# First two blocks of an attention and two-MoE kernel: another order, other engines, the first two steps in token halves, and identity transposes on an idle TensorE

## The chip, the core and the metric

The kernel runs on one core of a Trainium2 chip, in one launch. The metric is the device time of that launch in microseconds, the median of several runs. Five engines work beside each other, each through its own instructions in order: TensorE (PE), VectorE (DVE), ScalarE (ACT), GpSimd (POOL) and SyncE (SP), which here only issues DMA transfers. PE has a granted clock with two levels, 1.2 and 2.4 GHz; the profile gives it as a share of the higher one.

## The reference

```python
# q, k, v: [8, 8, 576, 64]; per chunk of 64 tokens and head:
scores = q_c @ k_c.T / sqrt(64); scores -= max; attn = exp(scores) / (sum + 1e-9); out = attn @ v_c
x  = out -> [4608, 512]
g  = relu(x @ w_in1)**2;  x1 = g @ w_out1                 # w_in [512, 2048], w_out [2048, 512]
h  = x1 @ w_in2
g2 = (a0 + a1*h + a2*h**2 + a3*h**3) / (1 + |b0|*|h| + |b1|*h**2 + 1e-6);  result = g2 @ w_out2
```

The four weight matrices arrive as 64-bit floats; the kernel loads the two 32-bit words of each and joins them to one 32-bit float.

## The kernel before, in words

The 4608 tokens are 36 attention tiles of 128 tokens and 9 blocks of 512 (4 tiles each). A block goes through 16 steps, one for each 128 columns of the hidden layer. A step `s` has a first product (`mm_h`, L181 to L183 through `mm3`): 12 matmuls of 128x512 into one of two PSUM banks of the pool `hps`; then ACT's Relu and Square (L227, L228), a rounded high part `gh` (L107, DVE) and the low rest `gl` (L110); and, some steps later, a second product (`mm_out1`): 12 matmuls of 128x512 into four `acc` banks. There are 12 because every 128x128 product is done as low x high, high x low and high x high. All 9 blocks pass the first MoE (144 steps), and then all pass the second.

Attention of tile t runs in between: q and k come in (`load_nat`, `load_tok` L253 for the first 8 tiles, `load_qk` L272 in units of 192 tokens and 16 + 16 small DMAs after them), are transposed (L290 with the identity, or L281 on DVE), then scores (`mm_s`, L314), maximum, subtraction, exponential, sum and division (L332 to L347; below: the chain of the tile), the transpose of the result (`f_tr`, L367), its copy out of PSUM (`f_copy`), the product with v (`mm_pv`, L323) and the high and low part of x (`x_evac`: L105, L110). For the first 8 tiles `f_tr`, the transposes of q and k and the scores share PSUM tiles of the pool `aps`; from the second block on this pool has a single tile `a`.

The first MoE's weights are made ready while block 0 and the attention of block 1 run. A weight tile (512 KB) goes through a load by SP (L131 for w_in, L135 for w_out) into a buffer `st`, two ACT operations on its words (L141, L143), a joining on DVE (L148) that frees `st`, a high part (`w_split`: L105 on ACT or L107 on POOL) and a low part on POOL (L110). The first 24 of the 32 tiles share 6 buffers `st`, the last 8 ("late") share 2. So a late load is issued only when the join two tiles before it is done, and behind whatever stands ahead of it in SP's row of DMAs.

What sets the order is a list of events with due times in steps of block 0, sorted, which gives each engine its program order; nothing is reordered after that. Times below 0 are the start: the string `order` lists tile by tile what tiles 0 to 3 do before step 0, and `load_nat` is given a list of loads. In the list `tq0` is the transpose of q of tile 0, `s0` its scores, `f0` its `f_tr`, `pv0` its product with v, `words0`, `join0`, `split0` the work on weight tile 0.

```python
    for i, x in enumerate("q0 k0 q1 k1 q2 k2 v0 q3 k3 v1 w0 v2 w1 v3 w2 w3 w4 q4 k4 w5 q5 k5".split()):
        at(-90 + i, load_nat, x)
```

Of the kernel before, what the change touches and what calls it, by code (L numbers as in the profile page):

```python
# [22 lines left out]
LN_SHIFT = 20  # L23


@with_exitstack
def attn_moe_moe_kernel(
# [60 lines left out]
    T = {}  # L88
    events = []

    def at(t, fn, *args):
        events.append((t, len(events), fn, args))
# [33 lines left out]
    def w_load(n, f, half):  # L126
        w = ((w_in1, w_out1), (w_in2, w_out2))[n][half]
# [10 lines left out]
    def w_words(key):  # L138
        st, pool_ = T[("st",) + key]
# [6 lines left out]
    def w_join(key):  # L146
        st, c = T.pop(("st",) + key)[0], T[("wc",) + key]
# [3 lines left out]
    def w_split(key, eng):  # L151
        _, f, half = key
# [5 lines left out]
    def w_keep(key):  # L158
        _, f, half = key
# [106 lines left out]
    def load_qk(u, src, nm, hp):  # L266
        t0, n = UNITS[u]
# [41 lines left out]
    def mm_s(t, key):  # L309
        q_, k_ = T.pop(("q", t)), T.pop(("k", t))  # L310
# [7 lines left out]
    def mm_pv(t, key):  # L318
        v_, a_ = T.pop(("v", t)), T.pop(("a", t))
        o = banks(T["aps", key], 1)  # L320
        for p in range(HP):
            for c, h in QUARTERS:
                nc.tensor.matmul(out=o[half(h), c, p], lhsT=v_[half(c), 2 * p + h], rhs=a_[h][half(c), :, p],  # L323
                                 start=True, stop=True)
        T["x", t] = o

    def s_max(t):
        m = tl("attn", [128, 32], F32, "m", f"m{t % 2}")[:, 0:2 * HP].rearrange("p (a b) -> p a b", a=2)
        x = T.pop(("s", t))
        T["e", t] = tl("attn", [128, HP, 2, D], F32, "e", f"e{t % 2}")  # L330
        e = T["e", t].rearrange("p b a j -> p a b j")
        nc.vector.tensor_reduce(out=m, in_=x, axis=AX.X, op=ALU.max)  # L332
        nc.vector.tensor_tensor(out=e, in0=x, in1=m.to_broadcast([128, 2, HP, D]), op=ALU.subtract)

    def s_exp(t):
        e = T["e", t]
        nc.scalar.activation(out=e, in_=e, func=ACTF.Exp, scale=scale)

    def s_sum(t):
        z = T["z", t] = tl("attn", [128, 32], F32, "z", f"z{t % 2}")[:, 0:2 * HP].rearrange("p (a b) -> p a b", a=2)  # L340
# [4 lines left out]
    def s_norm(t, eng):  # L345
        e, z = T["e", t].rearrange("p b a j -> p a b j"), T.pop(("z", t))
# [13 lines left out]
    def f_tr(t, pool_="hps"):  # L360
        e = T.pop(("e", t))
        if pool_ == "hps":
            o = h_p.tile([128, HP, 128], F32, name="h", tag="h")
        else:
            o = P["aps"].tile([128, 2, 512], F32, name="a", tag="a")[:, 0].rearrange("p (a j) -> p a j", a=HP)
        for p in range(HP):
            nc.tensor.transpose(out=o[:, p], in_=e[:, p].rearrange("p a j -> p (a j)"), identity=P["ident"])  # L367
        T["aT", t] = o

    def f_copy(t):  # L370
        o = T.pop(("aT", t))
        a = T["a", t] = [tl("attn", [128, 2, HP, 32], F32, "ah", f"at{h}") for h in range(2)]
        for h in range(2):
            for c in range(2):
                copy((nc.scalar, nc.vector)[h], a[h][half(c)].rearrange("p i b r -> p b i r"),
                     o[half(h), :, half(c)].rearrange("p b (i r) -> p b i r", i=2))

    def x_evac(t, eng):
        b, i = divmod(t, TPB)
        xh, xl = (z[:, :, i * 128:(i + 1) * 128].rearrange("p b (c i) -> p c b i", c=2) for z in X[b % 2])  # L380
        x = T.pop(("x", t))
        copy(nc.scalar, xh, x)
        split_lo(eng, xl, x, xh)
# [82 lines left out]
    for i, x in enumerate("q0 k0 q1 k1 q2 k2 v0 q3 k3 v1 w0 v2 w1 v3 w2 w3 w4 q4 k4 w5 q5 k5".split()):  # L466
# [3 lines left out]
    def first(x):  # L470
        nm, t = x[:-1], int(x[-1])
        if nm in ("tq", "tk"):
            tr_nat(t, nm[1] + "n", nm[1])
            tr_copy(t, nm[1], nc.scalar)
# [5 lines left out]
        elif nm in ("norm", "xe"):  # L480
            {"norm": s_norm, "xe": x_evac}[nm](t, {"norm": nc.gpsimd, "xe": nc.vector}[nm])
        elif nm == "split":
            w_split(w_keys[t], (nc.gpsimd, nc.scalar)[t])
        elif nm in ("words", "join"):
            {"words": w_words, "join": w_join}[nm](w_keys[t])
        else:
            {"max": s_max, "exp": s_exp, "sum": s_sum, "f": f_tr, "cp": f_copy}[nm](t)
# [10 lines left out]
    def attention(t, t0):  # L498
        if t < 2 * TPB:
            at(max(t0 - 2.1, 0.45), tr_second, t)  # L500
            at(max(t0 - 1.95, 0.6), tr_copy, t, "q", nc.vector)
            at(max(t0 - 1.95, 0.6), tr_copy, t, "k", nc.vector)
# [5 lines left out]
        at(t0 + 0.2, s_max, t)  # L508
        at(t0 + 0.45, s_exp, t)
# [14 lines left out]
    for t in range(TPB, NTILE + 1):  # L524
# [123 lines left out]
```

## Time and profile before

| | us |
|---|---|
| median of 3 runs (1686.88 to 1687.67) | 1687.42 |
| span of the profiled execution, first to last instruction | 1684.5 |
| PE busy in that span | 1647.5 (98%) |
| DVE, ACT, POOL busy | 1100.5, 927.7, 347.4 |
| first matmul of step 0 (128x512) | at 32.27 |
| mean granted clock of PE | 0.990 |

The span is the measured time less what lies before the first and after the last instruction. In the page's 40 slices PE reads 9 in every slice but the first, second, fourth and last, and the granted clock is below 1 only in the first slice of 42 us. So a reader looks first at where PE stands still or runs slowly, which is in the first 144 us, and there for what ended each wait.

### The profile page before, as it was taken

Reading aid. Unit: us, or ns where it says so; the run is one execution under the profiler, and the core shown is the slowest. Engines: PE = TensorE matmul, PEld = TensorE weight load, DVE = VectorE, ACT = ScalarE, POOL = GpSimd, SP = SyncE. Lnnn points to the kernel's source line nnn. Section 1 sums busy time; section 2 is a strip of 40 time slices with the busy share of each in tenths; the row PEclk is TensorE's granted clock in tenths of the full one; section 3 lists DMA queues with packets and bytes.
Section 4 is the critical chain, followed back from the end, with each engine's and each line's share of the span. In section 5 each row is a group of like instructions: output and inputs, shape, how many; then the busy total and the mean of one; then the engine's idle time right before and its main releaser. Section 6 shows DMA issues by size and latency. Waiting matters only on the chain.

```text
span 1684.5 us, 24455 instructions
## 1 busy us (share of the span) xinstructions
PE 1647.5 (98%) x9312; PEld 1349.8 (80%) x9312; DVE 1100.5 (65%) x1808; ACT 927.7 (55%) x1502; POOL 347.4 (21%) x282
## 2 busy tenths in 40 slices
PE   6898999999999999999999999999999999999998
PEld 5777888888788888888887788888888888888886
DVE  5765765565665556652107877777777777777776
ACT  5663333333333333322447777777777777777775
POOL 2441000000000000000574323232323232323222
PEclk7999999999999999999999999999999999999999
DMA  9644333334334252210431010101010101000000
GB/s 243 177 121 117 81 102 95 88 94 107 79 79 113 71 130 63 71 32 1 137 101 63 1 51 1 50 0 51 1 51 1 51 0 51 1 32 20 1 26 25
DMA packets 213190, 108.58 MB, mean 64 GB/s; under 512 B 182224, under 2 KB 182224, under 8 KB 211920
## 3 DMA queue, kind: packets, MB, share of 16 engines
q1 hardware_dynamic: 213072, 107.01, 23.5%
q8 instruction: 73, 1.20, 0.3%
q14 instruction: 45, 0.37, 0.1%
HBM read 79.69 MB, written 27.26 MB: 63 GB/s over the span
## 4 chain that ended last, share of the span: by engine, by line
PE 87%; DVE 2%; ACT 1%; DMA 0%; issue 0%; SPq 0%; POOLq 0%; POOL 0%; DVEq 0%; ACTq 0%
PE acc L181 15%; PE h L181 14%; PE h L183 14%; PE h L182 14%; PE acc L183 14%; PE acc L182 14%; PE a L323 1%; PE a L314 1%; DVE t L395 1%; DVE w L416 0%; DVE g L421 0%; DMA x2d<-ev 0%; DVE t L415 0%; ACT t L394 0%; ACT gh L105 0%
## 5 line engine op out<-in xcount | busy, mean ns | idle before, releaser
L181 PE MATMUL h<-x,w 128*128 128x512 f32 x1152 | 452.1, 392 | 3.3 <-DVE w L410 2.5
L182 PE MATMUL h<-x,w 128*128 128x512 f32 x1152 | 450.7, 391 | 0.0
L183 PE MATMUL h<-x,w 128*128 128x512 f32 x1152 | 450.1, 391 | 0.0
L110 POOL TENSOR_TENSOR gl<-g,gh 128x512 fp32r<-128x512 f32 x144 | 186.2, 1293 | 550.0 <-ACT gh L105 545.1
L227 ACT ACTIVATE r<-h 128x512 f32<-128x512 f32 x144 | 85.8, 596 | 384.0 <-PE h L183 362.2
L107 DVE CAST gh<-r 128x512 fp32r<-128x512 f32 x144 | 66.0, 458 | 312.1 <-ACT r L228 306.2
L181 PEld LDWEIGHTS h<-x,w 128*128 128x128 f32 x1152 | 217.5, 189 | 50.5 <-DVE w L410 4.5
L183 PEld LDWEIGHTS h<-x,w 128*128 128x128 f32 x1152 | 217.7, 189 | 45.7
L182 PEld LDWEIGHTS h<-x,w 128*128 128x128 f32 x1152 | 217.5, 189 | 45.4 <-DVE x L110 0.4
L181 PE MATMUL acc<-gh,w 128*128 128x512 f32 x576 | 228.8, 397 | 3.0 <-POOL w L110 2.1
L395 DVE SCALAR_TENSOR_TENSOR t<-h,co,t 128x512 f32<-128x512 f32 x144 | 125.4, 871 | 158.3 <-ACT t L394 158.3
L181 PE MATMUL acc<-w,gl 128*128 128x512 f32 x576 | 225.7, 392 | 1.8 <-POOL gl L110 1.8
L183 PE MATMUL acc<-gh,w 128*128 128x512 f32 x576 | 225.0, 391 | 0.0
L182 PE MATMUL acc<-gl,w 128*128 128x512 f32 x576 | 224.9, 390 | 0.0
L183 PE MATMUL acc<-w,gh 128*128 128x512 f32 x576 | 224.2, 389 | 0.0
L182 PE MATMUL acc<-w,gh 128*128 128x512 f32 x576 | 224.1, 389 | 0.0
L110 POOL TENSOR_TENSOR gl<-r,gh 128x512 fp32r<-128x512 f32 x16 | 20.7, 1291 | 681.4 <-DVE gh L107 681.4
L105 ACT ACTIVATE gh<-g 128x512 fp32r<-128x512 f32 x144 | 91.1, 633 | 89.4 <-DVE g L421 89.4
L181 PEld LDWEIGHTS acc<-w,gl 128*128 128x128 f32 x576 | 108.1, 188 | 28.7 <-POOL gl L110 2.6
L181 PEld LDWEIGHTS acc<-gh,w 128*128 128x128 f32 x576 | 108.4, 188 | 28.0 <-POOL w L110 2.3
L183 PEld LDWEIGHTS acc<-gh,w 128*128 128x128 f32 x576 | 108.4, 188 | 23.0
L183 PEld LDWEIGHTS acc<-w,gh 128*128 128x128 f32 x576 | 108.1, 188 | 22.7
(75 smaller groups left out, 2259.7 us busy)
## 6 DMA issues: line engine op xcount, KB each, us to landing
st<-in_moe_w_in_dram SPq DMA_DIRECT2D x32, 512.0 KB, 4.3
st<-in_moe_w_out_dram SPq DMA_DIRECT2D x32, 512.0 KB, 4.2
x2d<-ev SPq DMA_DIRECT2D x36, 256.0 KB, 2.4
x<-x2d SPq DMA_DIRECT2D x9, 1024.0 KB, 4.8
out_dram<-ev SPq DMA_DIRECT2D x36, 256.0 KB, 2.3
v<-in_v_dram SPq DMA_DIRECT2D x32, 256.0 KB, 3.9
w2d<-wc SPq DMA_DIRECT2D x32, 256.0 KB, 2.6
w<-w2d SPq DMA_DIRECT2D x32, 256.0 KB, 2.6
```

The costliest lines, as they stand in the source:

```text
L105: nc.scalar.activation(out=o, in_=x, func=ACTF.Copy)
L107: eng.tensor_copy(out=o, in_=x)
L110: eng.tensor_tensor(out=o, in0=x, in1=hi.bitcast(F32), op=ALU.subtract)
L181: nc.tensor.matmul(out=o, lhsT=al, rhs=bh, start=first and i == 0, stop=False)
L182: nc.tensor.matmul(out=o, lhsT=ah, rhs=bl, start=False, stop=False)
L183: nc.tensor.matmul(out=o, lhsT=ah, rhs=bh, start=False, stop=last and i == len(pairs) - 1)
L227: nc.scalar.activation(out=r, in_=ps, func=ACTF.Relu)
L314: nc.tensor.matmul(out=o[half(c), h, p], lhsT=q_[half(h), p, half(c)], rhs=k_[half(h), p, half(c)], start=True, stop=True)
L323: nc.tensor.matmul(out=o[half(h), c, p], lhsT=v_[half(c), 2 * p + h], rhs=a_[h][half(c), :, p], start=True, stop=True)
L395: nc.vector.scalar_tensor_tensor(out=t, in0=h2, scalar=co[:, 5:6], in1=t, op0=ALU.mult, op1=ALU.add)
```

## The change

- **Order of the start.** The string `order` is written anew: `max`, `sub`, `x_hi`, `x_lo` and the four pieces of `f_copy` become events of their own, with copies of tiles 0 to 3 on other engines (`ON`: "A" ACT, "V" DVE, "G" POOL). The loads are listed anew: v3 stands behind w2, q4, w4 and w5.
- **Halves.** Steps 0 and 1 compute `h` in two halves of 256 tokens (`mm_h_half`): the first halves need tiles 0 and 1 only, and stand before and after `pv3`.
- **Identity transposes.** `warm` puts 20 and then five times 8 transposes of the identity into an unused PSUM tile, between the first transposes of q and k.
- **f_tr.** For tiles 2 and 3 it is 16 products of 64x64 instead of 4 transposes of 128x128. For tiles 4 to 7 it goes into an `hps` bank instead of the tile `a`, and stands earlier among the steps (`t0 + 1.201` instead of `t0 + 1.9`).
- **Engines and due times.** The division of tiles 4 and 6 goes from DVE to POOL, that of tile 3 from POOL to DVE, some high parts and copies change engine, and 43 events (`MOVED`) get another due time, among them the load of the late tile w_out 13.

```diff
+ON = {
+    "cp000": "V", "cp010": "A", "cp110": "A", "cp111": "A", "cp300": "V", "cp401": "V", "cp501": "V",
...
+MOVED = {
+    "w_load:0,4,0": -11.296, "w_words:(0,2,0)": -11.499, "w_join:(0,2,0)": -11.4, "w_words:(0,0,1)": -12.5,
...
     def at(t, fn, *args):
-        events.append((t, len(events), fn, args))
+        key = fn.__name__ + ":" + ",".join(str(x).replace(" ", "") for x in args if isinstance(x, (int, str, tuple)))
+        events.append((t + MOVED.get(key, 0.0), len(events), fn, args))
...
+    def mm_h_half(s, i):
+        for j in range(2):
+            need("w", (0, j, 0), 4)
+            need("x", 2 * i + j, 3)
+        if i == 0:
+            T["h", s] = h_p.tile([128, 512], F32, name="h", tag="h")
+        j = slice(NB // 2 * i, NB // 2 * (i + 1))
+        mm3(T["h", s][:, j], [(w_in_cols(s, c), [X[0][p][:, c, j] for p in range(2)]) for c in range(KC)], True, True)
+
+    def warm(i, n):
+        if i == 0:
+            T["warm"] = P["aps"].tile([128, 2, 512], F32, name="a", tag="s2")
+        for j in range(n):
+            nc.tensor.transpose(out=T["warm"][:, 0, 0:128], in_=P["ident"], identity=P["ident"])
...
-    def f_tr(t, pool_="hps"):
+    def f_tr(t):
+        stage("softmax", t, 5)
         e = T.pop(("e", t))
-        if pool_ == "hps":
-            o = h_p.tile([128, HP, 128], F32, name="h", tag="h")
-        else:
-            o = P["aps"].tile([128, 2, 512], F32, name="a", tag="a")[:, 0].rearrange("p (a j) -> p a j", a=HP)
+        if on(f"fm{t}", "") is not None:
+            o = T["aps", t][:, :, 0:256].rearrange("p a (b j) -> p a b j", j=64)
...
+                        nc.tensor.matmul(lhsT=x, rhs=one, start=True, stop=True, **args)
+            T["aT", t] = o
+            return
+        if t < TPB:
+            o = T["aps", t][:, :, 0:256].rearrange("p a (b j) -> p a b j", j=128)
+        else:
+            o = h_p.tile([128, 512], F32, name="h", tag="h").rearrange("p (a b j) -> p a b j", a=2, j=128)
...
-    for i, x in enumerate("q0 k0 q1 k1 q2 k2 v0 q3 k3 v1 w0 v2 w1 v3 w2 w3 w4 q4 k4 w5 q5 k5".split()):
+    for i, x in enumerate("q0 k0 q1 k1 q2 k2 v0 q3 k3 v1 w0 v2 w1 w2 q4 w4 w5 v3 w3 k5 k4 q5".split()):
...
-    order = """tq0 tk0 s0 tq1 max0 exp0 tk1 s1 sum0 norm0 tq2 max1 tk2 f0 exp1 s2 sum1 norm1 cp0 tq3 pv0 tk3 max2 f1 xe0
-               exp2 sum2 norm2 cp1 s3 pv1 max3 xe1 f2 exp3 words0 sum3 norm3 cp2 join0 pv2 words1 f3 xe2 split0 cp3
-               join1 split1 pv3 xe3"""
+    order = """w020 tq0 w18 tk0 qc0 kc0 w28 s0 max0 tq1 sub0 w38 qc1 tk1 exp0 w48 kc1 s1 sum0 max1 norm0 sub1 tq2 qc2 exp1 f0
+               cp00 cp03 tk2 kc2 sum1 w58 cp01 s2 cp02 norm1 pv0 max2 sub2 xr0 xh0 xl0 tq3 qc3 exp2 f1 cp10 cp12
+               cp11 cp13 tk3 kc3 s3 sum2 max3 norm2 sub3 words0 xr1 pv1 xh1 join0 split0 xl1 exp3 words1 sum3
+               norm3 f2 cp20 cp22 cp21 cp23 join1 split1 pv2 xr2 xr3 xh2 f3 cp30 cp32 cp31 cp33 half00 pv3 xl2
+               half10 xh3 xl3"""
...
-            at(t0 + 0.8, s_norm, t, nc.vector)
-            at(t0 + 1.9, f_tr, t, "aps")
-            at(t0 + 1.95, f_copy, t)
+            at(t0 + 0.8, s_norm, t, on(f"norm{t}", "V"))
+            at(t0 + 1.201, f_tr, t)
...
     for s in range(NS):
-        at(s, mm_h, s)
+        if s < 2:
+            at(s, mm_h_half, s, 1)
+        else:
+            at(s, mm_h, s)
```

In `order`, `w020` is `warm(0, 20)`, `cp03` is the piece 3 of `f_copy` of tile 0, `half10` is the first half of step 1.

SP's row, the loads of the start before (`v` is the load of v of tiles 1, 2 and 3, `st` a weight tile):

```order
DMA v<-in_v_dram 128x8x64
DMA st<-in_moe_w_in_dram 128x2x512
DMA v<-in_v_dram 128x8x64
DMA st<-in_moe_w_in_dram 128x2x512
DMA v<-in_v_dram 128x8x64
DMA st<-in_moe_w_in_dram 128x2x512 x2
```

The same place after:

```order
DMA v<-in_v_dram 128x8x64
DMA st<-in_moe_w_in_dram 128x2x512
DMA v<-in_v_dram 128x8x64
DMA st<-in_moe_w_in_dram 128x2x512 x2
DMA qn<-in_q_dram 64x8x64 x2
DMA st<-in_moe_w_out_dram 128x1024 x2
DMA v<-in_v_dram 128x8x64
```

The load of v of tile 3 has moved from behind two weight tiles to behind five and q of tile 4.

PE's row around `f_tr` of tile 4 before; it stands behind the second product of step 1 (`w_1`), and writes the tile `a`:

```order
L181 MATMUL acc_516<-gh,w_1_91 128x512
L182 MATMUL acc_516<-gl,w_1_91 128x512
L183 MATMUL acc_516<-gh,w_1_91 128x512
L367 MATMUL a<-ident,e 128x128 x4
L181 MATMUL h<-x_69,w_4_80 128x512
```

After, it stands behind the first product of step 3, and writes an `hps` bank:

```order
L221 MATMUL h<-x_70,w_3_79 128x512
L222 MATMUL h<-x_69,w_3_79 128x512
L457 MATMUL h<-ident,e 128x128 x4
L353 MATMUL a<-ident,qn 128x128 x4
L353 MATMUL a<-ident,kn 128x128 x4
L220 MATMUL acc_621<-gh,w_1_91 128x512
```

So it comes one product of 12 matmuls earlier, ahead of the transposes of q and k of tile 5, which stood far ahead of it.

SP's row at the late weights before (`qs`, `ks` are the small loads of q and k of a unit, `st` of w_out the late tiles 11, 12 and 13 to 15):

```order
DMA qs<-in_q_dram 32x6x32 x4
DMA st<-in_moe_w_out_dram 128x1024
DMA qs<-in_q_dram 32x6x32 x12
DMA st<-in_moe_w_out_dram 128x1024
DMA ks<-in_k_dram 32x6x32 x16
DMA st<-in_moe_w_out_dram 128x1024 x3
```

The same place after:

```order
DMA qs<-in_q_dram 32x6x32 x4
DMA st<-in_moe_w_out_dram 128x1024
DMA qs<-in_q_dram 32x6x32 x8
DMA st<-in_moe_w_out_dram 128x1024
DMA ks<-in_k_dram 32x6x32 x4
DMA st<-in_moe_w_out_dram 128x1024
DMA ks<-in_k_dram 32x6x32 x12
DMA st<-in_moe_w_out_dram 128x1024 x2
```

Tile 12 stands behind 8 small loads instead of 12, and tile 13 behind 4 instead of 16; 12 of them now stand ahead of tile 14.

## Rows read from the trace of the kernel before

**Rows 1.** Stretches (us): length, busy and count by engine, granted clock, DMA share, GB/s.
```profile
0.00:10.00 10.00, 5.09 (x48) 3.94 (x48) 1.38 (x2) 3.09 (x5) 0.70 (x6) 1.00 0.92 178
10.00:20.00 10.00, 6.29 (x155) 5.03 (x154) 7.08 (x15) 6.05 (x13) 2.09 (x2) 1.00 1.03 256
20.00:30.00 10.00, 5.44 (x79) 3.88 (x73) 7.05 (x16) 5.43 (x11) 3.96 (x4) 0.52 1.00 249
30.00:40.00 10.00, 8.86 (x57) 7.02 (x58) 3.87 (x7) 7.18 (x13) 4.40 (x4) 0.63 1.03 293
144.00:880.00 736.00, 735.02 (x4840) 603.50 (x4839) 394.99 (x784) 248.68 (x424) 54.89 (x43) 1.00 0.34 86
```

**Rows 2.** Timeline, PE and POOL at the start: start, duration, engine, line, [idle before, releaser].
```profile
1.01 0.29 POOL masks.py:199 TENSOR_SCALAR_AFFINE_SELECT ident<-ident 128x128 f32<-128x128 f32 x1
4.21 1.09 PE L290 MATMUL h<-ident,qn 128*128 128x128 f32 x4 [4.21 <-DMA qn<-in_q_dram]
...
8.17 1.11 PE L290 MATMUL h<-ident,qn 128*128 128x128 f32 x4
9.08 1.06 PE L290 MATMUL h<-ident,kn 128*128 128x128 f32 x4
...
30.31 1.13 PE L323 MATMUL a<-ah,v 64*64 64x64 f32 x30 [0.83 <-DVE ah L107]
32.27 0.76 PE L181 MATMUL h<-x,w 128*128 128x512 f32 x1 [0.83 <-ACT x L105]
...
37.62 0.60 PE L290 MATMUL a<-ident,qn 128*128 128x128 f32 x4
38.06 0.60 PE L290 MATMUL a<-ident,kn 128*128 128x128 f32 x4
```

**Rows 3.** Timeline, PE, block 0 with the attention of tiles 4 to 8.
```profile
49.08 0.63 PE L290 MATMUL a<-ident,qn 128*128 128x128 f32 x4 [1.09 <-issue]
...
57.37 0.63 PE L367 MATMUL a<-ident,e 128*128 128x128 f32 x4 [1.76 <-DVE k L107]
...
79.27 0.63 PE L367 MATMUL a<-ident,e 128*128 128x128 f32 x4 [2.69 <-DVE k L107]
...
120.39 0.63 PE L367 MATMUL a<-ident,e 128*128 128x128 f32 x4 [1.08 <-ACT r L228]
123.08 0.79 PE L181 MATMUL acc<-gh,w 128*128 128x512 f32 x1 [2.06 <-POOL w L110]
...
126.22 0.40 PE L182 MATMUL acc<-gl,w 128*128 128x512 f32 x1
...
132.58 0.39 PE L183 MATMUL acc<-gh,w 128*128 128x512 f32 x1
137.16 1.14 PE L323 MATMUL a<-ah,v 64*64 64x64 f32 x32 [4.19 <-DVE ah L107]
138.89 1.13 PE L314 MATMUL a<-k,q 64*64 64x64 f32 x32 [0.60 <-DVE k L281]
...
143.42 0.40 PE L183 MATMUL h<-x,w 128*128 128x512 f32 x1
```

**Rows 4.** Timeline, SP's row of DMAs and ACT at the late weights.
```profile
120.67 7.64 SPq L272 DMA_DIRECT2D ks<-in_k_dram  x16
128.41 9.62 SPq L135 DMA_DIRECT2D st<-in_moe_w_out_dram  x3
...
132.49 0.66 ACT L141 ACTIVATE wc<-st 128x512 f32<-128x512 f32 x1 [5.66 <-DMA st<-in_moe_w_out_dram]
```

**Rows 5.** Timeline, scores (PE) and division (DVE) of tiles 5 and 6.
```profile
63.92 0.65 PE L314 MATMUL a<-k,q 64*64 64x64 f32 x32
76.03 0.69 DVE L347 TENSOR_TENSOR e<-e,z 128x512 f32<-128x512 f32 x1
88.53 0.65 PE L314 MATMUL a<-k,q 64*64 64x64 f32 x32
95.97 1.52 DVE L347 TENSOR_TENSOR e<-e,z 128x512 f32<-128x512 f32 x1
```

More of the change, by code (lines that the diff above doesn't have):

```diff
@@ L88, in attn_moe_moe_kernel, with on, stage, need @@
     T = {}
+    engines = {"A": nc.scalar, "V": nc.vector, "G": nc.gpsimd, "": None}
+    def on(what, usual):
+        return engines[ON.get(what, usual)]
     events = []
     def at(t, fn, *args):
-        events.append((t, len(events), fn, args))
+        key = fn.__name__ + ":" + ",".join(str(x).replace(" ", "") for x in args if isinstance(x, (int, str, tuple)))
+        events.append((t + MOVED.get(key, 0.0), len(events), fn, args))
+    done = {}
+    def stage(what, key, i):
+        if done.get((what, key), 0) != i:
+            raise ValueError(f"{what} {key}: stage {i} out of order")
+        done[what, key] = i + 1
+    def need(what, key, i):
+        if done.get((what, key), 0) < i:
+            raise ValueError(f"{what} {key} is not at stage {i}")
     def issue(until):
@@ L126, in w_load @@
     def w_load(n, f, half):
+        stage("w", (n, f, half), 0)
         w = ((w_in1, w_out1), (w_in2, w_out2))[n][half]
@@ L138, in w_words @@
     def w_words(key):
+        stage("w", key, 1)
         st, pool_ = T[("st",) + key]
@@ L151, in w_split @@
     def w_split(key, eng):
+        stage("w", key, 3)
         _, f, half = key
@@ L158, in w_keep @@
     def w_keep(key):
+        stage("w", key, 3)
         _, f, half = key
@@ L186, in mm_h @@
         b, f = divmod(s, NF)
+        if s < NS:
+            for i in range(2):
+                need("w", (0, f // 2 * 2 + i, 0), 4)
+            for i in range(TPB):
+                need("x", b * TPB + i, 3)
+        stage("h", s, 0)
         ps = h_p.tile([128, 512], F32, name="h", tag="h")
@@ L266, in load_qk @@
     def load_qk(u, src, nm, hp):
+        stage(nm, u, hp)
         t0, n = UNITS[u]
@@ L280, in tr @@
         for u, to, of, n in units(t):
+            need(nm, u, HP)
             nc.vector.transpose(
@@ L309, in mm_s @@
     def mm_s(t, key):
+        stage("s", t, 0)
         q_, k_ = T.pop(("q", t)), T.pop(("k", t))
@@ L318, in mm_pv @@
     def mm_pv(t, key):
+        if t < TPB:
+            for i in range(4):
+                stage(f"copy{i // 2}{i % 2}", t, 1)
+        else:
+            stage("softmax", t, 10 if t < 2 * TPB else 6)
         v_, a_ = T.pop(("v", t)), T.pop(("a", t))
@@ L368, in f_tr, with f_copy @@
         T["aT", t] = o
[L370 to L378, printed above, removed]
-        b, i = divmod(t, TPB)
[L380 to L383, printed above, removed]
+    def f_copy(t, h, c):
+        stage("softmax", t, 6 + (2 * h + c if t >= TPB else 0)) if t >= TPB else stage(f"copy{h}{c}", t, 0)
+        if on(f"fm{t}", "") is not None:
+            if h == 0 and c == 0:
+                a = tl("attn", [128, HP, 2, D], F32, "ah", f"at{t % 2}")
+                copy(on(f"cp{t}{h}{c}", "A"), a.rearrange("p (a b) h j -> p a (b h) j", a=2), T["aT", t])
+                T["a", t] = [a[:, :, h_] for h_ in range(2)]
+            return
+        if h == 0 and c == 0:
+            T["a", t] = [tl("attn", [128, HP, D], F32, "ah", f"at{h_}") for h_ in range(2)]
+        copy(on(f"cp{t}{h}{c}", "AV"[h]), T["a", t][h][half(c)].rearrange("p (a b) j -> p a b j", a=2),
+             T["aT", t][half(h), :, :, half(c)])
@@ new lines, in x_parts, with x_raw, x_hi @@
+    def x_parts(t):
+        b, i = divmod(t, TPB)
+        return [z[:, :, i * 128:(i + 1) * 128].rearrange("p b (c i) -> p c b i", c=2) for z in X[b % 2]]
+    def x_raw(t):
+        stage("x", t, 0)
+        if t >= 2 * TPB:
+            need("h", (t // TPB - 1) * NF - 1, 1)
+        if (eng := on(f"xr{t}", "")) is not None:
+            x = x_parts(t)[1].bitcast(F32)
+            copy(eng, x, T.pop(("x", t)))
+            T["x", t] = x
+    def x_hi(t):
+        stage("x", t, 1)
+        copy(on(f"xh{t}", "A"), x_parts(t)[0], T["x", t])
@@ L387, in t2, with x_lo @@
+    def x_lo(t):
+        stage("x", t, 2)
+        xh, xl = x_parts(t)
+        split_lo(on(f"xl{t}", "V"), xl, T.pop(("x", t)), xh)
     def t2(nm):
```

69 lines of the change are left out of this document (53 added, 16 removed), and 13 rows, old and new, of tables (MOVED, ON).

## The prediction, put down before the changed kernel ran

> **What bounds the kernel now.** I read the stretches first. From 144 to 880 us PE is busy 735.02 of 736 us at the full clock [rows 1], and nothing in the change touches what runs there. So the question is only when PE comes to the work that both kernels do alike from about 144 us on; each microsecond won or lost before that goes through to the end. Before 144 us the granted clock is about half from 20 to 30 us and 0.63 from 30 to 40 us [rows 1], and the timeline of PE shows where it waits.
>
> Of this I make a budget, from the first matmul of step 0 at 32.27 us on.
>
> Waits of PE [rows 2, 3], in the order of time: 1.09 (transposes of tile 5, which need the tile `a`), 1.76 and 2.69 (`f_tr` of tiles 4 and 5, held by the copy of k out of the same tile `a`), 1.08 (`f_tr` of tile 7), 2.06 (a late weight's low part on POOL), 4.19 (product with v of tile 7) and 0.60. Together 13.5 us.
>
> Slow clock. At the full level a 128x512 matmul takes (132.58 - 126.22) / 28 = 0.227 us, for 28 starts between these rows [rows 3]. The 12 matmuls of step 0 take 37.62 - 32.27 = 5.35 us [rows 2] where 12 x 0.227 = 2.73 would do: 2.6 lost. The seven from 123.08 to 126.22 take 3.14 against 1.59: 1.55 lost. From 137.16 to 143.42 pass 6.26 us, less 0.60 of waiting 5.66, for a product with v, scores and eight matmuls, which at the full level are about 2 x 0.6 + 1.8 = 3.0 [rows 3]: 2.6 lost. Together 6.8 us. Waits and slow clock after 32.27 us make 20.3 us: that is what can be won there.
>
> The longest wait shows where it comes from. SP issues 16 small loads of k for 7.64 us from 120.67 on, and only then w_out 13. ACT waits 5.66 us for that landing, until 132.49, and what stands behind it on ACT (Relu of a step, a copy of tile 7's transposed result) waits with it, and so the product with v at 137.16 [rows 3, 4].
>
> **The change part by part.**
>
> *The start.* Step 0 can't end before tile 3 has its product with v, and v3 now comes later. Ahead of and with v3 stand 13 loads of 256 KB and five of 512 KB, 6.0 MB. The queue moved 1.8 MB in the first 10 us, 2.6 in the next, and 2.5 in the third [rows 1]: v3 can't land before about 27 us. The new identity transposes cost something: the identity is there at 1.3 us, four transposes at the pace of 8 to 9 us take 9.08 - 8.17 = 0.91, so the first 20 end at 1.3 + 20 x 0.23 = 5.9 us and hold the first real ones, which started at 4.2, as soon as q0 had landed [rows 2]. Loads into the buffer of q0 wait for those. That moves the loads by up to 1.7 us. I take 29 us for v3, with 27 and 31 as ends. From its product with v to the first matmul of step 0 pass 32.27 - 30.31 = 1.96 us [rows 2], so the second half of step 0 starts at 31 (29 to 33). By then the first halves of steps 0 and 1 are done, in the time in which PE stood idle before: 12 x 0.227 = 2.73 us of work. Before, this point was 32.27 + 2.73 = 35.0. Won: 4.0 us (2 to 6). The other new work on PE there (40 identity transposes, 32 products of 64x64 in place of 8 transposes) lies in the stage that waits for loads and for the chain of the tiles; I cost it at nothing, and at its own 40 x 0.11 to 40 x 0.23 = 4 to 9 us if that cover were gone.
>
> *Halves.* 48 matmuls of 256 columns take the place of 24 of 512. No row shows one. A 128-column transpose has a pitch of (38.06 - 37.62) / 4 = 0.11 [rows 2], a 512-column one 0.227. Ends: half of 0.227, so nothing lost, or all of it, 24 x 0.114 = 2.7 us for the two halves behind the wait for tile 3. As a load of 128 columns of weights fits into 0.11, I take 0.12 and 0.4 us in all.
>
> *Clock at the start.* PE is slow from 20 us on because it has little to do, and rose again 3 to 6 us after it got dense work: at 37.6 after 32.27, at 126.2 after 123.08, at 143.4 after 137.16 [rows 2, 3]. The last eight identity transposes stand before the scores of tile 2, so nothing new fills the stretch in which the clock fell. The first halves start the dense work about 2 to 3 us earlier, partly under waits. At this level (1.2 GHz) the second halves would take 5.4 us instead of 2.7. I leave 1.5 us lost (0 to 2.6).
>
> TensorE: Matmul & The Clock Gate of the Trainium skill says (What's actually happening) that the throttled state is the default and activity releases it. By that rule more transposes are good anywhere in the start, and the 1.5 us would be 0. The trace agrees that dense work releases it, but shows the full level already at 38 us only and not where the transposes were added; the second rival below takes the rule's side.
>
> *f_tr of tiles 4 to 7.* It no longer needs the tile `a`, so the waits of 1.09, 1.76 and 2.69 lose their cause. But it comes earlier, so the chain of its tile must be done earlier; where it isn't, PE waits, and all products behind it with it. Before, the division of tile 5 ended at 76.72, 12.2 us after its scores (64.57), that of tile 6 at 97.49, 8.3 us after (89.18) [rows 5]. Now PE has, between scores and `f_tr`: for tile 4 three groups of 12 matmuls, 8.2 us; for tile 5 three and two transposes and a product with v, 9.5; for tile 6 two and the transposes, 6.3; for tile 7 two and a product with v, 6.0. The chains get shorter: DVE takes the maximum of tile 5 behind fewer joins, tile 6 loses a join (0.6) and its division goes to POOL. I work them out at about 7 to 8 us, so tile 6 waits 1.1 and the others little. For this, and for a wait for k4 (0.7) and for the first weight of the second product (0.5), which both come a little late when PE is 5 us ahead, I take 3 us (0 to 12).
>
> *Late weights.* w_out 13 now stands behind 4 small loads, 12 fewer, each 7.64 / 16 = 0.48: 5.7 us earlier, the length of ACT's wait [rows 4]. w_out 12 is 1.9 us earlier. Since SP sends the small loads also earlier where PE is ahead (the joins that free its buffers stand at the same place among the steps), I expect the 2.06, 4.19 and 0.60 gone, and with them the two slow stretches. What is late next is w_out 14, behind 12 small loads, 5.7 us; it is first used three groups later (8 us), so it is covered.
>
> **The sum.** 20.3 + 4.0 - 0.4 - 1.5 - 3 = 19.4 us. The profiled span of 1684.5 becomes 1665.1. The median of the runs is 2.9 above the span, so 1668. The most that the terms allow is 20.3 + 6 = 26.3 us, 1661; the least, with 12 us of new waits, 2.7 for the halves, 2.6 of slow clock and 2 won at the start, is 5 us, 1682, but not all of these ends come at once.
>
> **The rivals.**
>
> *New waits at f_tr.* If the chains keep their length, 8.3 to 12.2 us, mean 10.3, the four tiles wait 2.1, 2.7, 2.0 and 4.3 = 11 us in place of my 1.1. For it: DVE and ACT still run strictly by program order, and Relu and joins stand before the maximum. Against: the copies and joins that stood there are moved. Time: 1668 + 10 = 1678.
>
> *The transposes keep the clock up.* Then nothing is slow at the start: 1666.5. Against it: the clock had risen by 37 us and earlier without them, and fell where none is added.
>
> *Late weights come no earlier.* If SP, not PE, sets the pace of the late tiles, then 2.06 + 4.19 + 0.60 and the 4.2 of slow clock stay: 1668 + 11 = 1679. For it: the last tiles share two buffers. Against it: PE's first wait of 2.06 comes when these loads stand behind small ones, and that is what moves.
>
> *Slower: the two `hps` banks.* `f_tr` now takes one of the two banks, so the next first product needs the bank of the step just before, which ACT's Relu frees; and Relu stands in ACT's row behind words of weights that may not have landed. A wait like the one of 5.66 us [rows 4] would then stop PE directly. Four of these are 22.6 us in place of my 3. After the waits of 2.06 and 4.19 the clock fell, at 1.55 and 2.6 us; four times 2.1 make 8.4 more: 1668 - 3 + 22.6 + 8.4 = 1696. It decides where wait and slow clock together pass (19.4 + 3) / 4 = 5.6 us for each of the four tiles, a wait of 3.5 us. Against it: in block 0 the weights are loaded far ahead, so only the last two could meet it.
>
> **How the numbers follow.** Forecast 0.57; new waits at `f_tr` 0.19; clock kept up 0.08; late weights no earlier 0.08; slower by the banks 0.08. The time is that of the likeliest, 1668. The range holds the likeliest, the second and the third rival and all but the far end of the first: 1661 to 1680. This measurement can tell about 0.2% (3.4 us) from no change. Faster by more: nearly all of the first four cases, less 0.06 for cases that end near zero because several of the smaller terms go wrong together: 0.86. Within: 0.06. Slower: 0.08.
>
> **What would show it.** Right: in the profile after, the first matmul of 256 columns stands at 26 to 29 us and the second half of step 0 at 29 to 33; the waits of `f_tr` for the copy of k are gone; no wait of ACT for w_out over 2 us; no granted clock below 1 after 40 us; PE comes to the step that ran at 144 us about 20 us earlier. Wrong: waits of 2 us or more in front of the transposes of tiles 4 to 7 (first rival); a first product that waits for Relu (the last); ACT still waiting 5 us for w_out 13; or the second half of step 0 later than 34 us, since then the loads at the start were mis-sized.

## The result, and the profile after

The changed kernel takes 1670.74 us (median of 4 runs, 1670.36 to 1670.81) against 1687.15 for the kernel before beside it: a ratio of 0.9904 with a 95% interval from 0.9890 to 0.9918, 16.4 us less. The forecast was 1668 with a range from 1661 to 1680. The span of the profiled execution is 1668.9 us, 15.6 below the 1684.5 of before.

The page after: the span, the busy time, and the slices of PE and of its granted clock.

```profile
span 1668.9 us, 24673 instructions
...
PE 1649.8 (99%) x9436; PEld 1356.2 (81%) x9436; DVE 1101.5 (66%) x1806; ACT 923.9 (55%) x1494; POOL 353.4 (21%) x286
...
PE   8989999999999999999999999999999999999998
...
PEclk8999999999999999999999999999999999999999
```

A 9 in the row of the clock stands for 90% or more of a slice. The page of before has a 9 there for the slow stretches at 120 to 126 us (0.73) and 135 to 145 us (0.66) too, so its clock was below 1 in more than the first slice.

The same stretches as in [rows 1], columns as there:

```profile
20.00:30.00 10.00, 8.50 (x107) 7.60 (x97) 6.96 (x13) 6.42 (x12) 4.18 (x5) 0.56 1.14 270
30.00:40.00 10.00, 9.98 (x123) 9.12 (x123) 5.35 (x9) 7.62 (x14) 4.58 (x5) 0.93 1.12 283
144.00:880.00 736.00, 734.38 (x4835) 602.57 (x4833) 390.02 (x769) 252.33 (x429) 61.63 (x48) 1.00 0.34 86
```

From 144 to 880 us PE is as full as before: 734.38 of 736 us busy. What was won lies before. In this execution the clock is 0.93 from 30 to 40 us in place of 0.63; from 20 to 30 us it is still near half, though PE is now busy 8.50 us instead of 5.44.

Where the time came from is read off one mark that both kernels have, the scores of tiles 4 to 9 on PE (start, us, by the timelines):

| scores of tile | 4 | 5 | 6 | 7 | 8 | 9 |
|---|---|---|---|---|---|---|
| before | 41.61 | 63.92 | 88.53 | 110.27 | 138.89 | 161.26 |
| after | 37.47 | 57.09 | 79.44 | 101.61 | 124.00 | 145.08 |
| lead | 4.1 | 6.8 | 9.1 | 8.7 | 14.9 | 16.2 |

So 4.1 us come from the start, 5.0 from the stretch between the scores of tiles 4 and 6, and 7.5 from that of the late weights (tiles 7 to 9); 0.4 is lost between. Each row is one execution. Among the experiments below, the runs with the start of the kernel before have the scores of tile 4 at 41.6 to 43.0 us (five executions with this one), and those with the start of the changed kernel at 36.9 to 38.6 (six): in the mean the start is worth 4.4 us, and a single pair of profiles gives it only to within about 1.5 us.

The timeline of PE at the start (start, duration, line, [idle before, releaser]), with the half steps on L220 to L222:

```profile
1.36 3.76 PE L249 MATMUL a<-ident 128*128 128x128 f32 x20 [1.36 <-POOL ident masks.py:199]
4.96 0.60 PE L353 MATMUL h<-ident,qn 128*128 128x128 f32 x4
...
25.59 1.06 PE L447 MATMUL a<-ident,e 64*64 64x64 f32 x8
26.58 1.96 PE L449 MATMUL a<-ident,e 64*64 64x64 f32 x16
28.47 0.58 PE L220 MATMUL h<-x,w 128*128 128x256 f32 x1
...
30.99 0.41 PE L222 MATMUL h<-x,w 128*128 128x256 f32 x1
31.33 0.75 PE L392 MATMUL a<-ah,v 64*64 64x64 f32 x32
...
33.54 0.28 PE L220 MATMUL h<-x,w 128*128 128x256 f32 x1
...
34.86 0.28 PE L222 MATMUL h<-x,w 128*128 128x256 f32 x1
34.98 0.60 PE L353 MATMUL a<-ident,qn 128*128 128x128 f32 x4
...
37.47 0.69 PE L378 MATMUL a<-k,q 64*64 64x64 f32 x32
```

The first half of step 0 runs from 28.47, the product with v of tile 3 comes behind it at 31.33, and at 33.54, behind the first half of step 1, the second half of step 0 begins (forecast 29 to 33, so it is 0.5 us past the end of that range; the first half was forecast at 26 to 29). From 25.59 on PE doesn't wait for anything: it is busy with the 64x64 products and the half step, at half clock until about 31.4.

The waits of PE in block 0 with the attention of tiles 4 to 8, to be laid beside [rows 3]:

```profile
51.41 0.50 PE L220 MATMUL h<-x,w 128*128 128x512 f32 x1 [0.76 <-ACT r L288]
...
87.38 0.65 PE L457 MATMUL h<-ident,e 128*128 128x128 f32 x4 [0.75 <-POOL e L423]
...
110.36 0.63 PE L457 MATMUL h<-ident,e 128*128 128x128 f32 x4 [1.90 <-DVE e L423]
118.31 0.50 PE L220 MATMUL h<-x,w 128*128 128x512 f32 x1 [1.86 <-ACT r L288]
124.00 0.69 PE L378 MATMUL a<-k,q 64*64 64x64 f32 x32
```

All seven waits of [rows 3], 13.5 us, are gone; four new ones of 5.3 us stand there. Two are `f_tr` (L457) waiting for its tile's division, two are a first product (L220) waiting for Relu (L288), that is, for its `hps` bank. From 31.4 to 160 us the granted clock is 1.00 in this execution.

SP and ACT at the late weights, beside [rows 4]:

```profile
109.58 1.83 SPq L334 DMA_DIRECT2D ks<-in_k_dram  x4
111.51 0.39 SPq L170 DMA_DIRECT2D st<-in_moe_w_out_dram  x1
111.94 6.81 SPq L334 DMA_DIRECT2D ks<-in_k_dram  x12
118.84 2.27 SPq L170 DMA_DIRECT2D st<-in_moe_w_out_dram  x2
```

```profile
96.17 0.67 ACT L177 ACTIVATE wc<-st 128x512 f32<-128x512 f32 x1 [2.45 <-DMA st<-in_moe_w_out_dram]
...
116.56 0.67 ACT L177 ACTIVATE wc<-st 128x512 f32<-128x512 f32 x1 [1.99 <-DMA st<-in_moe_w_out_dram]
...
122.43 0.67 ACT L177 ACTIVATE wc<-st 128x512 f32<-128x512 f32 x1 [1.06 <-DMA st<-in_moe_w_out_dram]
```

The load of w_out 13 stands behind 4 small loads, and ACT's wait for it, at 116.56, has shrunk from 5.66 to 1.99 us.

### The profile page after: what moved, and what is told of

Same layout as the page of the kernel before. It is cut to its first block, busy times and chain, and to the rows that moved or that the text cites. A ratio compares the mean times of both kernels' runs of the same rounds, so it can differ in the third digit from the quotient of the medians.

```text
span 1668.9 us, 24673 instructions
## 1 busy us (share of the span) xinstructions
PE 1649.8 (99%) x9436; PEld 1356.2 (81%) x9436; DVE 1101.5 (66%) x1806; ACT 923.9 (55%) x1494; POOL 353.4 (21%) x286
## 4 chain that ended last, share of the span: by engine, by line
PE 91%; DVE 3%; ACT 2%; DMA 1%; SPq 1%; issue 1%; POOL 0%; POOLq 0%; DVEq 0%; ACTq 0%
PE acc L220 15%; PE h L220 15%; PE h L222 15%; PE h L221 15%; PE acc L222 14%; PE acc L221 14%; PE a L392 1%; SPq L334 1%; PE a L378 1%; DMA st<-in_moe_w_out_dram 1%; DVE t L506 1%; DVE w L527 1%; DVE g L532 0%; PE a L249 0%; DVE t L526 0%
## 5 line engine op out<-in xcount | busy, mean ns | idle before, releaser
L220 PE MATMUL h<-x,w 128*128 128x512 f32 (+1 forms) x1160 | 452.7, 390 | 5.1 <-ACT r L288 2.6
L221 PE MATMUL h<-x,w 128*128 128x512 f32 (+1 forms) x1160 | 450.8, 389 | 0.0
L222 PE MATMUL h<-x,w 128*128 128x512 f32 (+1 forms) x1160 | 450.7, 389 | 0.0
L288 ACT ACTIVATE r<-h 128x512 f32<-128x512 f32 x144 | 85.8, 596 | 383.6 <-PE h L222 361.3
L220 PEld LDWEIGHTS h<-x,w 128*128 128x128 f32 x1160 | 218.7, 188 | 52.6 <-DVE w L521 4.5
L222 PEld LDWEIGHTS h<-x,w 128*128 128x128 f32 x1160 | 218.8, 189 | 44.9
L220 PE MATMUL acc<-gh,w 128*128 128x512 f32 x576 | 228.0, 396 | 1.1 <-DVE ev L141 0.8
L220 PE MATMUL acc<-w,gl 128*128 128x512 f32 x576 | 225.7, 392 | 2.0 <-POOL gl L144 1.7
L222 PE MATMUL acc<-gh,w 128*128 128x512 f32 x576 | 224.5, 390 | 0.0
L222 PE MATMUL acc<-w,gh 128*128 128x512 f32 x576 | 224.2, 389 | 0.0
L220 PEld LDWEIGHTS acc<-w,gl 128*128 128x128 f32 x576 | 108.1, 188 | 29.2 <-issue 2.9
L220 PEld LDWEIGHTS acc<-gh,w 128*128 128x128 f32 x576 | 108.1, 188 | 25.7 <-DVE ev L141 1.6
L222 PEld LDWEIGHTS acc<-gh,w 128*128 128x128 f32 x576 | 108.1, 188 | 22.8
L222 PEld LDWEIGHTS acc<-w,gh 128*128 128x128 f32 x576 | 108.1, 188 | 22.6
```

Source lines behind the costliest of these rows:

```text
L220: nc.tensor.matmul(out=o, lhsT=al, rhs=bh, start=first and i == 0, stop=False)
L221: nc.tensor.matmul(out=o, lhsT=ah, rhs=bl, start=False, stop=False)
L222: nc.tensor.matmul(out=o, lhsT=ah, rhs=bh, start=False, stop=last and i == len(pairs) - 1)
L288: nc.scalar.activation(out=r, in_=ps, func=ACTF.Relu)
```

## The experiments

Each was timed beside the kernel before on the same chip (1686.4 to 1686.7 us); "of before" is the ratio with its interval. Differences from the changed kernel of less than about 2 us aren't resolved, since the changed kernel itself read 1670.74 and, repeated, 1671.51 us (0.9906 [0.9892, 0.9921]):

> The changed kernel once more, beside the others on the same chip: 1670 to 1672 by its first runs.

In the profile of the repeat, PE waits as long at `f_tr` of tile 7 as in the first one (1.90 there), but the wait of 1.86 us for Relu behind it isn't there:

```profile
110.78 0.63 PE L457 MATMUL h<-ident,e 128*128 128x128 f32 x4 [1.89 <-DVE e L423]
```

Instead the granted clock is 0.50 from 112 to 115 us.

**One: three due times of late loads taken out of the changed kernel.**

```diff
-    "load_qk:1,qs,0": -0.523, "load_qk:1,qs,1": -0.641, "w_load:0,13,1": -0.494,
```

> The changed kernel, with the three due times taken back that moved small loads of q and k of the second unit and the load of w_out 13: 16 small loads stand ahead of w_out 13 again. If the late weights' place in SP's row is what removed the waits behind w_out 13: w_out 13 is issued some 3 to 4 us later than at 111.5, ACT waits for it by so much more, PE waits 3 to 4 us more before a first product or a product with v, and the clock falls behind it: 1674 to 1677 us. If the pace of the late tiles is set elsewhere (the two buffers): within 1 us of 1670.7, since w_out 11 and 12 come about 2 us earlier in this order.

Measured: 1677.61, 0.9945 of before [0.9930, 0.9959], 6 to 7 us above the changed kernel and 0.6 above the expected range. The timeline of its PE and of its ACT:

```profile
123.17 0.80 PE L220 MATMUL h<-x,w 128*128 128x512 f32 x1 [8.33 <-ACT r L288]
```

```profile
121.43 0.66 ACT L177 ACTIVATE wc<-st 128x512 f32<-128x512 f32 x1 [6.89 <-DMA st<-in_moe_w_out_dram]
122.54 0.58 ACT L288 ACTIVATE r<-h 128x512 f32<-128x512 f32 x1
```

ACT waits 6.89 us for w_out, Relu stands behind it, and PE waits 8.33 us for the bank that Relu frees, 6.5 more than the 1.86 of the changed kernel, where 3 to 4 more were expected. The granted clock is 0.50 from 120 to 126 us. So the late loads are worth 6 to 7 us in the changed kernel, and the mechanism of the "slower" rival exists.

**Two: the same three due times alone, put into the kernel before.**

```diff
+        if fn.__name__ == "load_qk" and args[0] == 1 and args[2] == "qs" and args[3] < 2:
+            t -= (0.523, 0.641)[args[3]]
+        if fn.__name__ == "w_load" and args == (0, 13, 1):
+            t -= 0.494
```

> The kernel before, with the three due times alone that move eight small loads of q and the load of w_out 13. If these due times alone take away what I counted for the late weights (waits of 2.06, 4.19 and 0.60 and 4.2 of slow clock): 11 us faster, 1676. My own expectation after taking them back in the changed kernel (6.9 us): w_out 11 now stands behind four more small loads (1.9 us later) where it was already 2.06 us late, so 1.9 us are lost there and 4.19 + 0.60 + 2.6 won: 5.5 us faster, 1680 to 1683.

Measured: 1681.71, 0.9969 [0.9959, 0.9979]: 5.0 us faster.

**Three: the `hps` bank for `f_tr` of tiles 4 to 7 alone, in the kernel before, at the old place.**

```diff
-            at(t0 + 1.9, f_tr, t, "aps")
+            at(t0 + 1.9, f_tr, t)
```

> The kernel before, with f_tr of tiles 4 to 7 in an hps bank instead of the tile a, at its old place among the steps. If the copy of k out of the tile a is what held it: the waits of 1.76 and 2.69 go, 4.5 us, 1682 to 1683.5, and the clock and the late weights stay. If taking one of the two banks makes the first products wait for Relu for as long: 1686 or more, with waits of h for ACT's Relu of 2 us or more.

Measured: 1688.37, 1.0008 [0.9998, 1.0017]: nothing. The waits for the copy of k (1.76 and 2.69 us) are gone, and first products wait instead, as the timeline of PE shows:

```profile
58.66 0.77 PE L181 MATMUL h<-x,w 128*128 128x512 f32 x1 [2.38 <-ACT r L227]
...
79.89 0.50 PE L181 MATMUL h<-x,w 128*128 128x512 f32 x1 [0.55 <-ACT r L227]
...
133.67 0.79 PE L181 MATMUL h<-x,w 128*128 128x512 f32 x1 [5.88 <-ACT r L227]
```

Everything that the free tile `a` gave was given back at the bank.

**Four: both of these, and then the earlier place of `f_tr` as well** (`t0 + 1.201` for `t0 + 1.9`).

> The kernel before with the three earlier due times of late loads and with f_tr of tiles 4 to 7 in an hps bank, at its old place. By themselves they gave -5.0 and +1.6 us. First theory, they need each other (the bank's wait of 5.9 us at tile 7 was a Relu behind words of w_out 13, which now land earlier; and the copy of k no longer holds f_tr): 1676 to 1680, no wait of a first product for Relu over 3 us. Second theory, they add up: 1682.5 to 1685, with the 5.9 us still there or moved.

> The same, with f_tr of tiles 4 to 7 also at its new place (due 1.2 steps behind the scores), engines and joins as in the kernel before. First theory, the place needs the shorter chains that the other edits make: f_tr waits for the division of tiles 4 to 7 by 6 to 11 us together, and the time is 3 to 8 us above that of the run with the bank and the loads alone. Second theory, the place alone does it: waits at f_tr of 3 us or less, 1674 to 1678, and the rest of the change outside the start is worth 2 us or less.

Measured: 1681.51 (0.9969 [0.9957, 0.9980]) and 1681.84 (0.9973 [0.9963, 0.9983]), the same as the late loads alone. The first lies between the times of its two theories (1676 to 1680, 1682.5 to 1685): the 5.88 has become 0.87, as the first theory had it; but the wait at tile 4 stays, the clock is at its lower level behind it (0.50 from 60 to 62 us), and 1.71 (division of tile 7) and 2.07 (a late weight) come in. PE and then ACT of the first:

```profile
59.77 0.64 PE L185 MATMUL h<-x,w 128*128 128x512 f32 x1 [2.35 <-ACT r L231]
```

```profile
57.41 0.63 ACT L109 ACTIVATE w<-wc 128x512 fp32r<-128x512 f32 x1 [2.51 <-DVE wc L152]
...
59.06 0.57 ACT L231 ACTIVATE r<-h 128x512 f32<-128x512 f32 x1
```

Here Relu is late because ACT's row has the high part of a weight ahead of it, which waits 2.51 us for a joining on DVE. In the second kernel `f_tr` comes too early for the old chain of its tile; these waits come to 6.8 us, as its first theory had it, without the 3 to 8 us of time that it forecast (PE):

```profile
53.48 0.63 PE L371 MATMUL h<-ident,e 128*128 128x128 f32 x4 [2.96 <-DVE e L351]
...
120.83 0.63 PE L371 MATMUL h<-ident,e 128*128 128x128 f32 x4 [3.17 <-DVE e L351]
```

So neither bank nor place is worth anything without the other order and engines. What the bank is worth with them was not run: no run has the new order and engines with `f_tr` in the tile `a`. Against the changed kernel the second one is 4.5 us behind at the scores of tile 4 (41.99), loses 5.5 more up to those of tile 5 (67.07), and in each stretch after that the two differ by 0.7 us at most. Of these 5.5 us, 4.0 are two waits (2.96 above and 1.07 before the transposes of tile 5), and about 1.7 are an estimate for the clock, which is 0.50 from 54 to 57.4 us; the changed kernel has one wait of 0.76 us there.

**Five: only the place of `f_tr` undone in the changed kernel** (back to `t0 + 1.9`, in the `hps` bank, and without the four entries of `MOVED` for `f_tr` of tiles 4 and 6 and a copy of tiles 4 and 7).

> The changed kernel with f_tr of tiles 4 to 7 back at its old place (due 1.9 steps behind the scores in place of 1.2), still in an hps bank. First theory, the place is what lets the bank be free again: the waits for the division (0.75 and 1.90 us) go, but a first product now stands right behind f_tr of tiles 4, 5 and 7 or one group after it, and waits for Relu as in the kernel before with the bank alone (2.4, 0.6 and 5.9 us there): 1673 to 1677. Second theory, Relu is no longer behind words of weights, so the place is worth nothing: 1669 to 1671.5.

Measured: 1672.39, 0.9914 [0.9899, 0.9929]: 0.9 to 1.7 us above the changed kernel, not resolved, and between the ranges of the two theories. Its waits at the bank are 0.74 and 0.21 us, and one of 2.32 us for a late weight's low part comes in. The second theory is nearer: with the new engines the place is worth less than these runs resolve.

**Six: the halves undone, steps 0 and 1 whole.**

> The changed kernel with steps 0 and 1 as whole first products of 512 columns behind tile 3, as before. If the halves hide work in a stage in which PE has time: the product with v of tile 3 comes 2.5 us earlier, because the first half no longer stands before it, step 0 starts at about 31, and after it 2.7 us more of first products are to be done, part of them at the slow clock: 1672 to 1673.5. If the halves hide all their work: 2.7 us or more lost, over 1673.5. If PE was not what the second halves waited for: 1670.7.

Measured: 1672.60 (1670.31 to 1675.79), 0.9917 [0.9902, 0.9932]: 1.1 to 1.9 us above the changed kernel, not resolved. PE at the start:

```profile
30.27 1.13 PE L392 MATMUL a<-ah,v 64*64 64x64 f32 x32 [2.23 <-DMA v<-in_v_dram]
32.19 0.77 PE L220 MATMUL h<-x,w 128*128 128x512 f32 x1 [0.80 <-ACT x L139]
```

Without the first half in between, the product with v of tile 3 waits for its load, which landed at 30.2 us, and the scores of tile 4 come at 41.13. Against the profile of the changed kernel the halves are worth 3.7 us there (2.5 to 4.3 against the six executions of its start), of which 1.3 are left at the scores of tile 9 (146.35): a PE that comes later finds more of what it would wait for done, and waits 2.9 us in all between 33 and 160 us instead of 5.3.

**Seven: `f_tr` of tiles 2 and 3 as four transposes of 128x128 again** (`fm2` and `fm3` out of `ON`).

> The changed kernel, with four 128x128 transposes for f_tr of tiles 2 and 3 as before, in place of 16 products of 64x64. In the changed kernel these two groups hold PE for 2.5 and 2.9 us (21.01 to 23.5 and 25.59 to 28.47). If PE's slow work there holds the start: f_tr takes about 0.9 us each, the first halves start 2 to 3 us earlier, the second halves 1 to 2.5 us earlier, 1668.5 to 1669.7. If the four copies in place of one and the load of v3 (landed 27.43) hold it, or the clock rises later because PE does less: 1670 to 1672.

Measured: 1671.50, 0.9909 [0.9894, 0.9924]: no difference. PE:

```profile
26.67 1.13 PE L392 MATMUL a<-ah,v 64*64 64x64 f32 x32 [4.42 <-DVE ah L141]
27.73 1.11 PE L457 MATMUL a<-ident,e 128*128 128x128 f32 x4
```

`f_tr` of tile 3 now takes 1.11 us in place of 2.9, but the four copies out of PSUM that this form needs hold the product with v of tile 2 by 4.42 us (0.75 in the changed kernel), and the first half begins at 28.50. The longer form on PE buys one copy instead of four; the two are even within what these runs resolve.

**Eight: all 60 identity transposes out.**

> The changed kernel without its 60 identity transposes. If they only raise the clock from 4 us on instead of 10, while the first transposes start 0.75 us earlier without them, and the clock falls at about 20 us in any case: within 1 us of 1670.7. If they keep the clock up through the start (activity releases the throttle): the clock falls earlier or rises later than 31.4 us without them, and 2.6 us or more are lost: 1673 or more.

Measured: 1672.03 (1670.95 to 1674.99), 0.9910 [0.9894, 0.9927]: 0.5 to 1.3 us, not resolved. The stretches:

```profile
0.00:10.00 10.00, 5.10 (x48) 3.94 (x48) 1.67 (x3) 2.73 (x4) 0.70 (x6) 1.00 0.92 176
...
20.00:30.00 10.00, 8.49 (x125) 7.59 (x119) 7.22 (x14) 7.17 (x13) 4.21 (x4) 0.60 1.11 254
```

From 20 to 30 us the clock is 0.60 without them and 0.56 in the profile of the changed kernel, but that profile is the exception: its clock fell at 21.4 us (without them, at 22.1), while in the seven other executions that have the transposes it fell at 25.9 to 27.4 us. The same stretch in the repeat of the changed kernel:

```profile
20.00:30.00 10.00, 7.58 (x143) 6.77 (x134) 6.94 (x14) 6.38 (x12) 4.20 (x4) 0.81 1.05 267
```

In five executions with the start of before it reads 0.52 to 0.73. So the transposes may well keep the clock up longer; one run without them can't show it. It gains little: by 28 us the clock is 0.50 in every one of these executions, and the first half begins at 28.75 without them and at 27.95 to 28.75 with them.

**Nine: two attempts at the new waits.** In the first, `f_tr` of tiles 6 and 7 and the words of w_out 13 are due a little later; in the second, three late loads also move ahead of 4 small loads each.

```diff
-    "f_tr:6": -0.036, "f_copy:7,0,0": -0.501, "w_join:(0,13,1)": -0.149,
+    "f_tr:6": 0.1, "f_tr:7": 0.3, "w_words:(0,13,1)": 0.15, "w_split:(0,2,1)": 0.35, "w_join:(0,13,1)": -0.05,
+    "w_load:0,11,1": -0.5, "w_load:0,12,1": -0.2, "w_load:0,14,1": -0.7,    # second attempt only
```

> The changed kernel with f_tr of tiles 6 and 7 one group of 12 matmuls later, the words of w_out 13 behind Relu of step 13 and the high part of w_out 2 behind Relu of step 3. In the changed kernel PE waited 0.75 and 1.90 us at these f_tr and 0.76 and 1.86 us for Relu. If these waits are due to the place among the steps and on ACT: up to 5.3 us less, 1665.5 to 1667. If the time is given back at the late weights (PE then comes to them earlier than they land): 1668 to 1671, with new waits for POOL's low parts or for Relu after 110 us.

> The later f_tr of tiles 6 and 7 as in the run before it (1669.8), and three late loads earlier in SP's row: w_out 11 ahead of 4 small loads of q, w_out 12 ahead of 4, w_out 14 ahead of 4 small loads of k. If the waits of 2.3 and 2.2 us that came in place of those at f_tr are there because the words of w_out 11, 14 and 15 land late, both shrink to under 1 us: 1666 to 1668. If the two buffers of the late tiles hold them (SP waits for the join two tiles before), nothing moves: 1669 to 1670.5, and small loads of q and k behind them come later, which would show as a wait at the scores of tile 8.

Measured: 1669.80 (0.9896 [0.9879, 0.9912]) and 1668.56 (0.9891 [0.9876, 0.9906]). In the first the waits at `f_tr` of tiles 6 and 7 and for Relu go, and two of 2.3 and 2.2 us for late weights and what follows them come, as its second theory had it. In the second, the waits of PE from 33 to 160 us (view of waits: total, times, longest) are down to 2.2 us:

```profile
PE acc L220 <- POOL w L144: 1.4, 1, 1.4
PE h L457 <- DVE e L423: 0.6, 1, 0.6
PE h L221 <- DVE x L144: 0.2, 1, 0.2
```

Its time is 0.6 us over the range of its first theory: of the two waits one is gone and the other is still 1.4 us.

The second is the fastest kernel measured here, 2 to 3 us below the changed one at the median; the intervals overlap, so that it beats it is likely and not shown.

## Why the prediction was right, and where it was off

The mechanism held: the end of the program is set by when PE reaches the work behind 144 us, and the lead at the scores of tile 9, 16.2 us, is the gain. The sum of 19.4 was 3.0 too high:

| term | forecast | measured | from |
|---|---|---|---|
| old waits and slow clock after 32.27 us | 20.3 | 20.3 | none of them is left |
| start, less slow clock left there | 4.0 - 1.5 | 1.5 - 0 | 35.0 - 33.54; clock 1.00 from 31.4 on |
| halves | -0.4 | -0.1 | 24 x 0.119 - 2.73, the pitch (start to start) being (34.86 - 33.54) / 11 = 0.12 as taken |
| new waits | -3 | -5.3 | 0.76 + 0.75 + 1.90 + 1.86 |
| sum | 19.4 | 16.4 | |

That the column adds up to the 16.4 us of the medians is in part luck. It is read from one execution of each kernel; in the others with the same start, the second half of step 0 begins at 32.8 to 34.7 us, and step 0 of the kernel before at 32.3 to 33.5.

*The start.* This is the step that failed, by its size. I let the second half of step 0 follow the product with v of tile 3 by 1.96 us and that product follow its load, and I costed the new work on PE at nothing, under the cover of waiting for loads. v3 landed inside its bounds, at 27.4 (issue at 18.70, 8.7 us to landing, by the view of the tile `v`), but its product came only at 31.33, without a wait for the load: `f_tr` of tile 3 in the 64x64 form (2.9 us) and the half step (12 matmuls, 2.5 us at a pitch of 0.21) stood ahead of it on PE, both at half clock. The cover had ended at 25.59. I had taken the first half for work in an idle place; at half clock it was long enough to become the path. In the five other executions of this start the load landed at 29.7 to 30.9 and its product came 0.3 to 1.1 us later, again without a wait, so there load and half step end nearly together. That the load binds without the half step, and that four copies bind without the 64x64 form, is what six and seven show: the start has three paths within a few microseconds of each other, and each of these edits by itself moved the time by less than these runs resolve. The slow stretch that I left at 1.5 us past this point was not there; it had been paid before it.

*New waits.* The one at tile 6 was named (1.1 forecast, 0.75 measured), those for k4 and the first weight didn't show, and tile 7 was missed: 1.90 us for its division, and 1.86 us behind it, because `f_tr` of tile 7 holds one bank until its copies are done, the next first product needs the other, and Relu for that one stands behind words of w_out 13 that ACT waits 1.99 us for. This is the last rival's mechanism, which I had put at "only the last two could meet it"; here the last one does, and behind it the clock held. In the repeat it fell to 0.50 behind the wait of 1.89 us at the same `f_tr`, so the sign "no granted clock below 1 after 40 us" held in the first execution only.

The first rival, that the tiles' chains keep their length and `f_tr` waits 11 us, is refuted for this kernel, where `f_tr` waits 2.7 us; with the old engines it is right in kind, since there the waits for the division came to 6.8 us (view of waits, second kernel of four).

*Late weights.* As forecast: 2.06, 4.19 and 0.60 are gone with both slow stretches, and ACT's wait for w_out 13 fell from 5.66 to 1.99 us; one of 2.45 us for an earlier tile is over the 2 us that I allowed, and PE doesn't feel it. One and two put a price on it of 5.0 us in the kernel before and 6 to 7 in the changed one, where the third rival had 11 for it (6.85 of waits and 4.2 of slow clock): by themselves the three due times leave a wait of 3.08 us for w_out's low part in the kernel before. That it is more in the changed kernel is likely due to the bank, which makes PE wait for the same Relu directly (the 8.33 us in one). The rival that these tiles come no earlier is refuted.

*`f_tr` and the bank.* The waits for the copy of k went, as said. That their removal wins 5.5 us was right only with the other edits: three and four give nothing for bank and place. The last of them lies 5.5 us behind the changed kernel between the scores of tiles 4 and 5 (the same figure as the forecast's by chance: that one covers the waits up to tile 6), and its longest wait there is for the division of tile 4. What removes this must be the changed engines and order (the division of tiles 4 and 6 on POOL, the copy of k on ACT, Relu ahead of the high part that waits for a joining): this is by subtraction, since these moves were not tried by themselves. With it stays open how the some 10 us that the late loads don't explain divide among the new start, the engines and the bank.

*The clock.* The second rival fell in its outcome: with the transposes the clock still went to 0.50, at 21.4 us in the first profile and at 25.9 to 27.4 us in the seven others that have them, and it was there when the first half of step 0 ran. TensorE: Matmul & The Clock Gate of the Trainium skill (What's actually happening) has it that activity releases the lower level; by that rule the first 20 transposes should do it, and the trace agrees: the first four real transposes take 0.60 us instead of 1.09 [rows 2]. In seven other executions they take 0.60 to 1.06 us, and the eight identity transposes behind them run at the full pace (1.04 us) in all but one, where they take 1.15. But the start was waiting for loads then, and eight shows no gain of time beyond what these runs resolve.

## What to carry to other kernels

An edit that fills an idle place is free only as long as the place stays idle at the clock that rules there: work out its length at the lower level, and ask what stands behind it on the same engine. When a short-lived tile is moved from a crowded PSUM tile into a pool of two banks, the wait moves to whoever frees the other bank, and in these runs that paid nothing as long as this engine had something slow ahead of it. Where several paths end within a few microseconds, taking back single edits can measure as nothing (six, seven and eight) though the stage gained some 4 us; price the stage, not the edit. And read a start from more than one execution: the point at which the clock fell moved here by 5 us or more between executions of the same work.

## What the runs showed of the hardware

- Transposes alone raise PE's clock: 20 identity transposes from 1.36 us take 3.76 to 4.53 us in eight executions, and the eight behind the first real ones (at 5.4 to 6.5 us) take 1.04 us, or 1.15 in one of them; without them four transposes still take 1.06 us at 13.74 and 0.66 only at 16.98. The granted clock in the stretch from 0 to 10 us reads 1.00 with and without them, so at the very start the durations tell more than that column.
- A 256-column matmul keeps a pitch of 0.119 us at the full level and 0.214 at the lower one; a 512-column one keeps 0.227 and 0.427 (33.85 to 36.41 us in six). So two halves cost 5% more than the whole at the full level and nothing more at the lower one.
- Eight 64x64 products with the identity, recorded as 16 matmuls, take 1.96 us at the lower level and the eight 64x64 transposes beside them 1.06, against 1.11 for the four 128x128 transposes that the two groups replace. Here a transposing product takes nearly twice a transpose of its size.
- The same wait need not have the same effect on the clock: behind a wait of 1.90 us at `f_tr` of tile 7 the granted clock stayed at 1.00 in one execution of the changed kernel, and behind one of 1.89 us at the same place it was 0.50 from 112 to 115 us in another.
